# Strassen sums of a second weight matrix made earlier and kept in DRAM, left sums moved to another engine, and another order of seven products

## The chip, the cores and the metric

The kernel runs on one core of one Trainium2 chip. The metric is the device time of one execution in microseconds (us). Engines are named as the profile names them: PE is TensorE (PEld its weight loads), DVE is VectorE, ACT is ScalarE, POOL is GpSimd, SP is SyncE, which here issues nearly all DMAs.

## What is computed

```python
def rmsnorm(x, g):                                  # over the last axis
    return x / np.sqrt(np.mean(x * x, -1, keepdims=True) + 1e-06) * g
q_n, k_n = rmsnorm(q, g_q), rmsnorm(k, g_k)         # q, k, v: (8, 12, 448, 64) float32
attn = softmax(q_n @ k_n.transpose(0, 1, 3, 2) / 8)
x = (attn @ v).transpose(0, 2, 1, 3).reshape(3584, 768)
h = np.maximum(x @ moe_w_in, 0.0)                   # moe_w_in: (768, 2048)
out = (h * h) @ moe_w_out                           # moe_w_out: (2048, 768)
```

Everything is float32. The change concerns the last line, the product with `moe_w_out`, called the out product below, and in it the sums of its right operand (the out weights) and of its left operand (`h * h`).

## The kernel before

**Units.** The eight batches are handled in four units of two. The program runs attention for one unit while it runs the feed-forward of the unit before it, and the last unit's feed-forward runs alone at the end. Unit 0 also brings the weights in and makes their sums. Units 1 and 2 are the middle units (`KEPT`); unit 3 is the last.

**Out product by seven products.** The out product is computed by the Strassen-Winograd scheme: a product of two 2x2 block matrices takes seven block products P1 to P7 instead of eight, at the price of sums of blocks. Left operands are the blocks 11, 12, 21, 22 and the sums S1 to S4, right operands the blocks 11, 12, 21, 22 and T1 = 12 - 11, T2 = 22 - T1, T3 = 22 - 12, T4 = T2 - 21. `PRODUCTS` (line 946) says which left meets which right, and into which PSUM role it goes. The eight right forms of every pair of weight tiles are made once, during unit 0, and kept in DRAM as `out_forms[t]` (one for each of eight tiles), in rows of 384 columns.

**Middle units.** In units 1 and 2 the out product is done once for each of four blocks of the hidden dimension, with one level of the scheme, in `second_products` (line 1230). Its inner loop (line 1315) runs over `SPLIT_ORDER`, 21 products of two matmuls of 128x384. The weights lie in two `out_sb` tiles, loaded by `load_out` (line 924) a few at a time after the block before. Between the products the program goes back to `run` (line 1859), which at each step issues a few of the attention tasks: `tasks` for several engines, `pool_tasks` for POOL (sums of softmax weights, scaling of q, forms of the next unit), DMAs in `transfers`, and in `follow_loads` (line 1805) those DMAs whose count of steps has run out (`later`, `forms_to_load`). Each engine executes its own instructions strictly in the order in which the program issued them, SP its DMAs too. Six accumulators `accs` are allocated for a middle unit, of the seven buffers that the pool has.

**The last unit.** `last_unit` (line 1353) uses the scheme twice, one level inside the other. The outer level is `ROUNDS` (line 1340): seven rounds, one for each outer product, each with one right form (in the order 11, 21, T1, T2, 22, T3, T4), and the plain product with 12 at the end. A round has two half-rounds (`pair` 0 and 1, for two sets of token rows). Each half-round is again seven products, in the order of `ROUND_ORDER` (line 1344), each of four matmuls of 128x192 (line 1578) that go over the four blocks. So each round needs

- the right form, loaded by `load_right` (line 1382) from `out_forms` into `rights[n % 2]` in eight DMAs, issued when the round two before has ended;
- its inner sums, made by `sum_right` (line 1391): T1, T2 and T4 in `more_rights[n % 2]` and T3 in place of the block 12, four subtractions of 768 elements per partition on POOL. The first three are issued at the beginning of the second half of the round before, the fourth at the beginning of the round;
- its outer left sum, if its left operand is one, made a round ahead by `sum_left` (line 1435; which sum in which round says `MADE_IN`): two operations of 1024 elements on VectorE for half 0, two on POOL for half 1, all issued during half 0;
- four inner left sums for every half-round, made by `sum_second` (line 1463) on VectorE, 512 elements each, during the half-round before, one behind each product from the second on.

Each half-round uses three PSUM banks `a, b, c` of one of two sets. P1, P6 and P7 accumulate into a quarter `u_ps` in bank a, P2 goes to the first half of bank b, P5 and P3 to the second half `v_ps` of the same bank, and P4 to bank c. `put` (line 1468) adds a result to an accumulator in SBUF: after P1, P5, P6 and P4 a quarter (192 columns), after P3 the whole of bank b (384), after P7 two quarters at once. The rests, those rows that belong to no half, are done by `multiply_rest` (line 1477) as plain products of 16 records each at the beginning of rounds 0, 1, 4 and at the end. `finish_round` (line 1516) adds two accumulators on POOL after rounds 4 and 5 and stores finished columns; these stores stand in SP's queue with the loads of the right forms.

Of the kernel before, what the change touches and what calls it, by code (L numbers as in the profile page):

```python
# [14 lines left out]
F32 = mybir.dt.float32  # L15
# [8 lines left out]
P = 128  # L24
# [201 lines left out]
def program(ctx, tc, rows, v, g, wide, ones, moe_w_in, moe_w_out, out, shift):  # L226

    nc = tc.nc
# [5 lines left out]
    NF = DFF // P  # L234
    NK = NC // 2
    HALF = DM // 2
# [729 lines left out]
    assert len(KEPT) == 2  # L966
    kept = {u: dram.tile([NBLK, P, 2, 2, P], F32, name=f"rests{u}") for u in KEPT}
# [262 lines left out]
    def second_products(u, blk, hid, sums_, accs):  # L1230

        split = u in KEPT
        if blk == 0:
            accs.extend(new_acc() for _ in range(2 * NT if split else 2 * NT + 1))
# [109 lines left out]
    ROUND_ORDER = ["P1", "P5", "P2", "P6", "P4", "P3", "P7"]  # L1344
# [8 lines left out]
    def last_unit():  # L1353
# [28 lines left out]
        def load_right(n):  # L1382
            if n < len(ROUNDS):
                k = OUT.index(ROUNDS[n][1])
                for t in range(NF // 2):
                    nc.sync.dma_start(rights[n % 2][:, t], out_forms[t][:, k])
# [48 lines left out]
        def sum_left(name, pair, part):  # L1435

            one, other, op = LEFT_SUMS[name]
            engine = nc.gpsimd if pair else nc.vector
            if pair:
                dst, le, ri = [left_of(x, pair, part) for x in (name, one, other)]  # L1440
            else:
                dst, le, ri = [
                    (tokens(x, pair, slice(0, 2 * P)) if x in RAW else summed(x, pair))[:, :, part]
                    for x in (name, one, other)
                ]
            engine.tensor_tensor(out=dst, in0=le, in1=ri, op=op)  # L1446
# [86 lines left out]
        for n, (name, right) in enumerate(ROUNDS):  # L1533
# [9 lines left out]
            sum_right(n, 3)  # L1543
            yield COST_OUT
            for pair in range(2):
# [16 lines left out]
                if pair == 0 and n in MADE_IN:  # L1562
                    extra = deque(partial(sum_left, MADE_IN[n], 0, t) for t in range(2))
                    for t in range(2):
                        sum_left(MADE_IN[n], 1, t)
                else:
# [617 lines left out]
```

## Time and profile before

| what | value |
|---|---|
| median of 3 runs | 1381.4 us (1379.86 to 1383.52) |
| the profiled execution's own time | 1385.1 us |
| its span, first to last instruction | 1383.2 us |
| PE busy | 1344.0 us (97%), 6656 matmul records |
| DVE / ACT / POOL busy | 863.2 / 611.8 / 831.9 us |
| mean granted TensorE clock | 0.995 |
| DMA traffic | 229.88 MB, mean 166 GB/s |
| units 1 and 2, second products and attention among them | 489 to 1090 us |
| rounds of the last unit | 1212.8 to 1371.7 us |

How to read it: one execution on the chip was recorded by the hardware profiler. In the timeline a row has the start, the length, the engine, the line of the kernel, the operation, output and inputs by the program's names, the shapes and how many instructions were merged; in square brackets the idle time of that engine before it and who ended it. A float32 matmul of this kernel shows as two records, so a product of four matmuls is eight records. In a table of stretches each row has the length, the busy time of PE, PEld, DVE, ACT and POOL with their numbers of instructions, the granted clock, the DMA share and GB/s. In the list of waits a row says who waited for whom, for how long in total, how often, and the longest.

### The profile page before, as it was taken

What the parts mean: (1) busy time and instruction counts of PE and PEld (TensorE: products, weight loads), DVE (VectorE), ACT (ScalarE), POOL (GpSimd) and SP (SyncE); (2) the same over time, 40 slices, a digit from 0 to 9 for tenths busy, and PEclk for the clock granted to TensorE, in tenths of its full rate; (3) what the DMA queues carried; (4) which work ended last, traced back from release to release, by engine and by line L of the source; (5) the groups of instructions that cost most, each with busy time, mean ns of one, the idle gap of its engine ahead of it and who ended that gap; (6) DMA issues with size and microseconds to landing.
All of it is one profiled execution on the core that took longest, in us unless ns stands there. A gap on an engine that the chain in (4) does not pass through costs nothing.

```text
span 1383.2 us, 20325 instructions
## 1 busy us (share of the span) xinstructions
PE 1344.0 (97%) x6656; PEld 891.3 (64%) x6656; DVE 863.2 (62%) x1657; ACT 611.8 (44%) x1134; POOL 831.9 (60%) x784
## 2 busy tenths in 40 slices
PE   7999999999999999999999999999999999999897
PEld 3333444444444476776767585766767799978797
DVE  4897555877767765455557665555546645448674
ACT  6985477757756244442534244434424044410000
POOL 5668664746656888566767876665837413146451
PEclk9999999999999999999999999999999999999999
DMA  5665846968769866575649575656535464342222
GB/s 136 165 188 150 204 117 161 260 184 216 239 148 279 244 172 202 153 201 127 206 100 264 148 220 136 181 168 153 166 99 199 137 213 153 96 132 69 91 81 89
DMA packets 399928, 229.88 MB, mean 166 GB/s; under 512 B 272324, under 2 KB 366660, under 8 KB 398788
## 3 DMA queue, kind: packets, MB, share of 16 engines
q1 hardware_dynamic: 399520, 228.41, 58.9%
q8 instruction: 55, 0.90, 0.3%
q14 instruction: 61, 0.50, 0.1%
q10 hardware_dynamic: 292, 0.07, 0.0%
HBM read 171.05 MB, written 57.34 MB: 165 GB/s over the span
## 4 chain that ended last, share of the span: by engine, by line
PE 83%; DVE 6%; issue 3%; POOL 3%; ACT 2%; DMA 2%; SPq 1%; POOLq 0%; ACTq 0%; DVEq 0%
PE bank L1075 25%; PE bank L1272 20%; PE bank L1014 8%; PE bank L1578 8%; PE bank L567 4%; PE bank L449 4%; PE bank L460 4%; PE bank L552 3%; PE bank L1481 1%; PE bank L588 1%; DMA in_sb<-in_deep 1%; PE bank L1214 1%; PE bank L631 1%; DVE left_sums L1446 1%; PE bank L604 1%
## 5 line engine op out<-in xcount | busy, mean ns | idle before, releaser
L1075 PE MATMUL bank<-xT,in_sb 128*128 128x224 f32 x1344 | 287.0, 353 | 0.0
L1075 PEld LDWEIGHTS bank<-xT,in_sb 128*128 128x128 f32 x1344 | 253.1, 190 | 9.4 <-ACT wT L468 5.6
L468 ACT ACTIVATE wT<-bank,rr 128x448 f32<-128x448 f32 x288 | 163.8, 631 | 159.2 <-PE bank L449 98.4
L1272 PE MATMUL bank<-out_sb,hid 128*128 128x384 f32 x576 | 205.6, 489 | 2.1 <-POOL out_sb L1784 1.4
L204 POOL TENSOR_TENSOR rr<-ms,minus_half 128x8 f32<-128x8 f32 (+1 forms) x96 | 145.2, 1512 | 71.5 <-DVE ms L197 61.0
L1615 DVE TENSOR_TENSOR acc<-acc,bank 128x384 f32<-128x384 f32 x231 | 122.5, 546 | 97.8 <-PE bank L1272 77.6
L1272 PEld LDWEIGHTS bank<-out_sb,hid 128*128 128x128 f32 x576 | 108.1, 190 | 80.5 <-issue 7.0
L1272 PE MATMUL bank<-out_sb,sums 128*128 128x384 f32 x432 | 156.0, 491 | 1.4 <-DVE acc L1615 1.0
L1014 PE MATMUL bank<-xT,in_sb 128*128 128x448 f32 x336 | 131.8, 546 | 0.0
L1272 PEld LDWEIGHTS bank<-out_sb,sums 128*128 128x128 f32 x432 | 80.3, 190 | 67.1 <-issue 4.1
L487 POOL TENSOR_TENSOR sum<-sum,wT 128x448 f32<-128x448 f32 (+1 forms) x96 | 112.3, 1191 | 7.5 <-ACT wT L468 6.0
L1014 PEld LDWEIGHTS bank<-xT,in_sb 128*128 128x128 f32 x336 | 62.1, 190 | 68.8 <-issue 61.7
L460 PE MATMUL bank<-qT,kT 64*128 64x448 f32 (+1 forms) x492 | 102.6, 573 | 3.6 <-ACT qT L382 2.5
L1058 DVE TENSOR_TENSOR hid<-hid,bank 128x224 f32<-128x224 f32 x208 | 73.4, 382 | 43.9 <-PE bank L1075 40.5
L487 POOL TENSOR_TENSOR sum<-wT 128x448 f32<-128x448 f32 x48 | 55.9, 1184 | 69.1 <-ACT wT L468 69.1
L460 PEld LDWEIGHTS bank<-qT,kT 64*128 64x128 f32 (+1 forms) x492 | 35.4, 167 | 63.8 <-issue 35.1
L1075 PE MATMUL bank<-more,in_sb 128*128 128x224 f32 x288 | 74.4, 354 | 0.8 <-DVE whole_hid L1058 0.8
L449 PE MATMUL bank<-qT,kT 64*64 64x448 f32 x552 | 75.1, 540 | 0.0
L567 PE MATMUL bank<-wT,vt 64*64 64x448 f32 x576 | 73.3, 545 | 0.0
L382 ACT ACTIVATE qT<-qT,g 128x448 f32<-128x448 f32 x34 | 22.7, 666 | 110.1 <-DVE qT L372 110.1
L1678 ACT ACTIVATE words<-words 128x384 f16<-128x384 f32 x64 | 68.5, 1070 | 2.0
L1058 DVE TENSOR_TENSOR whole_hid<-whole_hid,bank 128x224 f32<-128x224 f32 x104 | 37.9, 386 | 37.1 <-PE bank L1075 35.1
(201 smaller groups left out, 2421.6 us busy)
## 6 DMA issues: line engine op xcount, KB each, us to landing
in_sb<-in_deep SPq DMA_DIRECT2D x64, 384.0 KB, 3.6
in_sb<-in_deep SPq DMA_DIRECT2D x80, 256.0 KB, 3.9
out_sb<-out_forms SPq DMA_DIRECT2D x48, 384.0 KB, 5.2
words<-in_moe_w_in_dram SPq DMA_DIRECT2D x32, 384.0 KB, 3.8
words<-in_moe_w_out_dram SPq DMA_DIRECT2D x32, 384.0 KB, 3.5
out_forms<-out_sb SPq DMA_DIRECT2D x8, 1536.0 KB, 6.6
right<-out_forms SPq DMA_DIRECT2D x64, 192.0 KB, 4.1
qk<-in_q_dram SPq DMA_DIRECT2D x96, 96.0 KB, 2.5
```

The source lines that it names most:

```text
L204: self.nc.gpsimd.tensor_tensor(out=self.rr[i][:, x, 0 : self.count(i)], in0=ms, in1=self.minus_half.to_broadcast(list(ms.shape)), op=ALU.pow,)
L449: nc.tensor.matmul(sc[ds(half * D, D)], lhsT=turned[i, 1][ds(e * D, D), ds(m * P + half * D, D)], rhs=turned[i, 0][ds(e * D, D), :], start ...
L460: nc.tensor.matmul(sc[some], lhsT=turned[p, 1][r, keys], rhs=turned[p, 0][r, :], start=True, stop=True,)
L468: nc.scalar.activation(new_weights((i, m), e), sc, AF.Exp, scale=rows.rr[i][:, 1, 2 * m + e : 2 * m + e + 1],)
L487: nc.gpsimd.tensor_tensor(out=sums[i, e][some], in0=left[some], in1=weights[key_of(i, m), e][some], op=ALU.add)
L567: nc.tensor.matmul(bank[ds(e * D, D), :], lhsT=values[i][keys, n, e, :], rhs=weights[(i, n), e][keys], start=n == 0, stop=n == NJ - 1 and ...
L1014: nc.tensor.matmul(ps, lhsT=w_sb[:, IN.index(left), c, :], rhs=forms[u, c][right], start=first and c == 0, stop=c == NK - 1, skip_group_ch ...
L1058: nc.vector.tensor_tensor(out=quarter(blk, name, n), in0=quarter(blk, base, n), in1=ps, op=ALU.add)
L1075: nc.tensor.matmul(ps, lhsT=left, rhs=right, start=start, stop=stop, skip_group_check=True)
L1272: nc.tensor.matmul(ps, lhsT=lefts[left][:, t, ts(tt, P)], rhs=w_sb[t][:, OUT.index(right), :], start=first and t == 0, stop=t == 1, skip_g ...
L1578: nc.tensor.matmul(ps, lhsT=left[l][:, blk], rhs=rest_of[r][:, blk], start=blk == 0 and product in ("P1", "P5", "P4"), stop=blk == NBLK - ...
L1615: nc.vector.tensor_tensor(out=acc, in0=acc, in1=ps, op=ALU.add)
```

## The change

In the middle units POOL now makes inner sums of the right forms, between the products of a block, and SP stores them in a new DRAM tile `second_forms`: unit 1 does T1 to T4 (four sums for four forms at a time), unit 2 does 21 and 22 (the first three sums for two forms). Each is a subtraction from the `out_sb` tiles into a seventh accumulator buffer, `made`, issued ahead of products 6, 10, 14 and 18 of the order, and its store is issued three steps later. `made` is one buffer, used by all of them in turn.

In the last unit `load_right` loads these sums instead of their being made: three DMAs into `more_rights`, and for T1 to T4 a fourth into the place of the block 12, whose own loads become half as long. POOL's `sum_right` stays for the form 11 (three sums, during the products before the rounds), and the fourth sum of 11, 21 and 22 is made on VectorE. `sum_left` is done on VectorE for both halves, in four pieces of 512 elements per half-round, in the same list of jobs as `sum_second`; two jobs are issued behind a product where the list is too long for one. And `ROUND_ORDER` has P4 and P2 exchanged.

```diff
+    second_forms = dram.tile([P, 8, 4, NBLK, HALF // 2], F32, name="second_forms")
...
-            accs.extend(new_acc() for _ in range(2 * NT if split else 2 * NT + 1))
+            accs.extend(new_acc() for _ in range(2 * NT + 1))
...
+        def sum_second_forms(n):
+
+            q = HALF // 2
+            some = (ds(4, 4), ds(2, 2))[KEPT.index(u)]
+            size = (4, 2)[KEPT.index(u)]
+            made = accs[-1][:, 0 : size * q].rearrange("p (k c) -> p k c", k=size)
+            b11, b12, b21, b22 = [w[:, some, ts(h, q)] for w in w_sb for h in range(2)]
+            left, right = ((b12, b11), (b22, made), (made, b21), (b22, b12))[n]
+            less(nc.gpsimd, made, left, right)()
+            later.append([3, partial(nc.sync.dma_start, second_forms[:, some, n, blk], made)])
...
-            for name, tt, n in SPLIT_ORDER:
+            for at, (name, tt, n) in enumerate(SPLIT_ORDER):
+                if at in (6, 10, 14, 18)[: 4 if u == KEPT[0] else 3]:
+                    sum_second_forms((at - 6) // 4)
...
-    ROUND_ORDER = ["P1", "P5", "P2", "P6", "P4", "P3", "P7"]
+    ROUND_ORDER = ["P1", "P5", "P4", "P6", "P2", "P3", "P7"]
...
         def load_right(n):
-            if n < len(ROUNDS):
-                k = OUT.index(ROUNDS[n][1])
-                for t in range(NF // 2):
-                    nc.sync.dma_start(rights[n % 2][:, t], out_forms[t][:, k])
+            if n >= len(ROUNDS):
+                return
+            name = ROUNDS[n][1]
+            k, to = OUT.index(name), rights[n % 2]
+            for t in range(NF // 2):
+                some = slice(0, HALF if t % 2 or name in RAW else Q)
+                nc.sync.dma_start(to[:, t, some], out_forms[t][:, k, some])
+            if name in ("11", "12"):
+                return
+            for m in range(3):
+                nc.sync.dma_start(more_rights[n % 2][:, m], second_forms[:, k, m])
+            if name not in RAW:
+                nc.sync.dma_start(right_of(n, 0, 1), second_forms[:, k, 3])
...
-            less(nc.gpsimd, dst, left, right)()
+            less(nc.vector if m == 3 else nc.gpsimd, dst, left, right)()
...
-        def sum_left(name, pair, part):
-
+        def sum_left(name, pair, i, t):
             one, other, op = LEFT_SUMS[name]
...
+            dst, le, ri = [left_of(x, pair, i)[:, :, t] for x in (name, one, other)]
+            nc.vector.tensor_tensor(out=dst, in0=le, in1=ri, op=op)
...
-            sum_right(n, 3)
+            if right in RAW:
+                sum_right(n, 3)
...
-                if pair == 0 and n in MADE_IN:
-                    extra = deque(partial(sum_left, MADE_IN[n], 0, t) for t in range(2))
-                    for t in range(2):
-                        sum_left(MADE_IN[n], 1, t)
-                else:
-                    extra = deque()
-                if pair and n + 2 < len(ROUNDS):
-                    for m in range(3):
-                        sum_right(n + 1, m)
-                for product in ROUND_ORDER:
+                if n in MADE_IN:
+                    jobs.extend(
+                        partial(sum_left, MADE_IN[n], pair, i, t) for i in range(2) for t in range(2)
+                    )
+                for slot, product in enumerate(ROUND_ORDER):
...
-                    if extra:
-                        extra.popleft()()
-                    elif jobs and product != "P1":
-                        jobs.popleft()()
+                    for _ in range(2 if len(jobs) > 6 - slot + 1 else 1):
+                        if jobs:
+                            jobs.popleft()()
```

More of the change, by code (lines that the diff above doesn't have):

```diff
@@ L1433, in left_of @@
             return tokens(name, pair, some)
-        def sum_left(name, pair, part):
+        def sum_left(name, pair, i, t):
             one, other, op = LEFT_SUMS[name]
-            engine = nc.gpsimd if pair else nc.vector
-            if pair:
-                dst, le, ri = [left_of(x, pair, part) for x in (name, one, other)]
-            else:
[L1442 to L1446, printed above, removed]
+            dst, le, ri = [left_of(x, pair, i)[:, :, t] for x in (name, one, other)]
+            nc.vector.tensor_tensor(out=dst, in0=le, in1=ri, op=op)
         rounds = [(n, pair) for n in range(len(ROUNDS) - 1) for pair in range(2)]
@@ L1561, in last_unit @@
                     jobs.extend(partial(sum_second, at + 1, x) for x in LEFT_SUMS)
-                if pair == 0 and n in MADE_IN:
-                    extra = deque(partial(sum_left, MADE_IN[n], 0, t) for t in range(2))
-                    for t in range(2):
-                        sum_left(MADE_IN[n], 1, t)
-                else:
-                    extra = deque()
-                if pair and n + 2 < len(ROUNDS):
-                    for m in range(3):
-                        sum_right(n + 1, m)
-                for product in ROUND_ORDER:
+                if n in MADE_IN:
[3 more added lines that the diff above has]
+                for slot, product in enumerate(ROUND_ORDER):
                     role, first, l, r = PRODUCTS[product]
```

## The prediction

> **What bounds the kernel now.** I read the page first, then the stretches and TensorE's waits of the two middle units, then the last unit in order of time.
>
> ```profile
> PE 1344.0 (97%) x6656; PEld 891.3 (64%) x6656; DVE 863.2 (62%) x1657; ACT 611.8 (44%) x1134; POOL 831.9 (60%) x784
> ```
>
> TensorE is busy in 1344.0 of 1383.2 us. An edit pays only where TensorE is idle or slow, and costs only where it makes TensorE wait. The middle units (489 to 1090 us) first: the stretches (length, then busy time of each engine; the sum is over 16 of them) and everything TensorE waited for there.
>
> ```profile
> 753.00:789.50 36.50, 35.73 (x157) 19.33 (x159) 27.52 (x49) 11.10 (x21) 31.75 (x38) 1.00 0.64 181
> ...
> sum 593.60, PE 591.15 PEld 418.63 DVE 338.92 ACT 232.50 POOL 406.14; mean PE 36.95 PEld 26.16 DVE 21.18 ACT 14.53 POOL 25.38
> ```
>
> ```profile
> PE bank L1075 <- DVE hid L1058: 1.2, 3, 0.6
> PE bank L1272 <- DVE acc L1615: 0.6, 1, 0.6
> PE bank L1272 <- ACT acc L1611: 0.4, 2, 0.2
> ```
>
> TensorE is idle for 593.60 - 591.15 = 2.45 us there, and never because of POOL. Nothing can be won in the middle units; something can be lost.
>
> Now the last unit's seven rounds: 14 half-rounds of seven products, each product four matmuls, which the trace shows as eight records. This sum row covers the three stretches in which only they run (the whole-row products of L1481 cut out):
>
> ```profile
> sum 148.59, PE 135.96 PEld 131.82 DVE 106.09 ACT 5.62 POOL 79.49; mean PE 45.32 PEld 43.94 DVE 35.36 ACT 1.87 POOL 26.50
> ```
>
> A slow half-round and an ordinary one, TensorE in order of time (start, length, what ended an idle time before it):
>
> ```profile
> 1237.53 1.46 PE L1578 MATMUL bank<-right,whole_hid 128*128 128x192 f32 x8
> 1238.83 1.46 PE L1578 MATMUL bank<-more_right,qk 128*128 128x192 f32 x8
> 1242.63 2.93 PE L1578 MATMUL bank<-right,whole_hid 128*128 128x192 f32 x8 [2.34 <-DVE acc L1475]
> 1245.35 1.78 PE L1578 MATMUL bank<-more_right,qk 128*128 128x192 f32 x8
> ...
> 1342.29 1.46 PE L1578 MATMUL bank<-right,left_sums 128*128 128x192 f32 x8
> 1343.59 1.46 PE L1578 MATMUL bank<-more_right,second_sums 128*128 128x192 f32 x8
> 1345.50 1.57 PE L1578 MATMUL bank<-right,left_sums 128*128 128x192 f32 x8 [0.45 <-DVE acc L1475]
> 1346.90 1.46 PE L1578 MATMUL bank<-more_right,second_sums 128*128 128x192 f32 x8
> ...
> 1352.10 1.46 PE L1578 MATMUL bank<-right,whole_hid 128*128 128x192 f32 x8
> ```
>
> One product takes 1343.59 - 1342.29 = 1.30 us, so seven take 9.12 (7 x 1.302). The ordinary half-round takes 1352.10 - 1342.29 = 9.81. The missing 0.69 lies at the third product, P2, which starts 1345.50 - 1343.59 = 1.91 after P5 instead of 1.30, and is itself 0.1 slow. P2 writes the first half of the bank whose second half P5 has just filled, and starts only when VectorE has emptied that half. In the slow half-round the same P2 starts 3.80 us after P5, for the reason that VectorE's rows show:
>
> ```profile
> 1239.30 3.02 DVE L1446 TENSOR_TENSOR left_sums<-whole_hid,whole_hid 128x1024 f32<-128x1024 f32 x1
> 1242.24 0.34 DVE L1475 TENSOR_TENSOR acc<-acc,bank 128x192 f32<-128x192 f32 x1
> ...
> 1286.33 1.21 DVE L1446 TENSOR_TENSOR left_sums<-whole_hid,left_sums 128x1024 f32<-128x1024 f32 x1
> 1287.47 0.34 DVE L1475 TENSOR_TENSOR acc<-acc,bank 128x192 f32<-128x192 f32 x1
> ...
> 1340.16 0.68 DVE L1466 TENSOR_TENSOR second_sums<-left_sums 128x512 f32<-128x512 f32 x1
> 1341.19 0.55 DVE L1475 TENSOR_TENSOR acc<-acc,bank 128x384 f32<-128x384 f32 x1 [0.34 <-PE bank L1578]
> ```
>
> ```profile
> 1237.13 1.80 POOL L744 TENSOR_TENSOR right<-right 128x768 f32<-128x768 f32 x1 [15.57 <-PE bank L1481]
> 1238.89 2.34 POOL L1446 TENSOR_TENSOR left_sums<-whole_hid,whole_hid 128x1024 f32<-128x1024 f32 x1
> 1241.20 3.32 POOL L1446 TENSOR_TENSOR left_sums<-rest_left,rest_left 128x1024 f32<-128x1024 f32 x1
> ```
>
> The eviction that P2 needs (1242.24) stands behind a left sum of 1024 elements, and that sum takes 3.02 us while POOL works on its own left sums, against 1.21 (1286.33) while POOL rests. The evictions themselves, with one input from PSUM, take 0.34 both times. And a long gap costs twice:
>
> ```profile
> 1242.60:1246.90 4.30, 4.27 (x16) 4.27 (x17) 4.30 (x2) 0.00 (x0) 4.30 (x2) 0.61 0.02 4
> ```
>
> After the gap of 2.34 us the granted clock is 0.61 for 4.3 us: P2 takes 1245.35 - 1242.63 = 2.72 instead of 1.30, and the next product is 1.78 long instead of 1.46, together about 1.7 us lost behind the gap.
>
> **Part by part.** *The order (P1, P5, P4, P6, P2, P3, P7).* P4 has a bank of its own, so the third product waits for nothing. P6 adds to P1's bank, P2 to P5's; each now has two products (2.60 us) between it and the fill of its bank, where P2 had none. P7 keeps two behind P6. If VectorE empties P1's and P5's quarters within 2.60 us of their end, all seven products run without a gap: 14 x 9.12 = 127.7 us in place of 148.59, which is 20.9 us less. Of this, 14 x 0.69 = 9.7 is the order alone, and 11.2 are the slow half-rounds.
>
> *VectorE's new load.* In the eight half-rounds of rounds 1 to 4 it gets four left sums of 512 elements beside its four second-level sums of 512 (0.68 each, row 1340.16). With four small evictions at 0.34 and two of 0.55 that is 8 x 0.68 + 1.36 + 1.10 = 7.9 us of 9.12; in the other six 5.2. In order, counted from the start of P1: the last eviction and job of the half-round before end at 1.4, P1's eviction at 1.9 (needed at 3.9), two sums by 3.2, P5's at 3.6 (needed at 5.2), a sum by 4.2, P4's by 4.6, a sum by 5.2, P6's at 5.8 (needed at 7.8). Every one is early by 1.6 us or more. The one subtraction on the right operand that stays (rounds 0, 1, 4) goes from POOL to VectorE: 768 elements, by the 512 row about 1.0 us. It waits for L1481 to have read that operand; behind it on VectorE are only evictions of products that start after L1481. It costs nothing; its result is due at P7, 7.8 us later.
>
> *POOL in the last unit* loses its left sums and all but the first three right sums, so the 3.02 us of row 1239.30 should fall to the undisturbed price. Four additions of accumulators stay, and each may hold one VectorE sum for some 1.8 us (row 1237.13 has the same size); the 1.6 us margin above nearly takes that. I set it at nothing.
>
> *Loads of the right operand.* Per round before:
>
> ```profile
> 1231.63 3.65 SPq L1386 DMA_DIRECT2D right<-out_forms  x8
> ```
>
> ```profile
> right<-out_forms SPq DMA_DIRECT2D x8, 192.0 KB, 3.8
> ```
>
> Eight issues in 3.65 us, the last landing 3.8 later: 1.57 MB in 7.5 us. After, a round of T1 to T4 brings 4 x 192 + 4 x 96 + 4 x 384 KB = 2.75 MB in 12 issues, one of 21 or 22 brings 2.75 MB in 11. At the same rate that is 13.1 us. They start when the round two before ends and are due one whole round, 18.2 us, later. 5 us to spare: no cost.
>
> *The middle units.* POOL gets 4 x 4 subtractions of 768 elements (1.80, row 1237.13) and 4 x 3 of 384 (half of that): 28.8 + 10.8 = 39.6 us. Each result is stored by SP, and each next one waits for that store, since all use one buffer. Behind a waiting subtraction on POOL stand the scaling of keys, the sums of the softmax weights and the forms for the next unit; behind a store that waits for POOL on SP stand loads of q, k, v, in_sb and out_sb. Who waits for those at last is TensorE. Over the 16 stretches POOL is idle for 593.60 - 406.14 = 187 us, so most of it fits. The tightest place is the end of unit 1:
>
> ```profile
> 774.19 0.93 POOL L643 COPY few<-few 32x14 f32<-32x14 f32 x4 [3.22 <-DVE few L641]
> ...
> 792.35 2.84 POOL L744 TENSOR_TENSOR xT<-xT 128x224 f32<-128x224 f32 x3
> ```
>
> ```profile
> 800.61 0.54 PE L1075 MATMUL bank<-more,in_sb 128*128 128x224 f32 x2
> ```
>
> ```profile
> out_sb<-out_forms SPq DMA_DIRECT2D x48, 384.0 KB, 5.2
> ```
>
> POOL has 36.50 - 31.75 = 4.75 us idle in that block; four subtractions are 7.2, so its forms come at least 2.5 us later. They are done at 795.2 at the latest and read at 800.61: 5.4 us of slack. No wait there is the low end. If the three waits for stores (5.2 us as a block of 384 KB, 0.4 to issue) were all uncovered, the lag would be 2.5 + 16.8 = 19.3 and TensorE would stand 13.9 us: the high end. A gain is excluded, as TensorE never waits for POOL there. Other POOL work lies between the subtractions and covers most of each store, so I stay by the first row: 1.5 us in all for the eight blocks.
>
> Sum: -20.9 + 1.5 = -19.4 us. The profiled execution took 1385.1 (span 1383.2); it would take 1365.7. It lies 3.7 above the median, so against the median of 1381.4: 1362.0.
>
> **The rivals.** *A stall between the units:* POOL's lag passes the slack by 5 us at one place. Priced by the row of the clock, such a gap adds 1.7 us behind it: 6.7 more than the sum without middle costs, 1360.5 + 6.7 = 1367.2, and twice that is 1373.9. For it: POOL's 31.75 of 36.50. Against: slack 5.4. The Trainium skill ("TensorE: Matmul & The Clock Gate", What's actually happening) has the clock fall only after an idle window of about 3.4 us; the row shows it at 0.61 after 2.34, so the measurement decides. By that rule a stall under 3.4 us would cost its own length alone.
>
> *VectorE becomes the bound:* if the eight fuller half-rounds take 10.5 instead of 9.12 (sums at 1.0 instead of 0.68), 8 x 1.4 = 11.2 of the gain is gone: 1373.2. Against it stands the undisturbed 0.68.
>
> *The order does not do it:* the wait moves from P2 to P6 or P2 at its new place, 14 x 0.69 = 9.7 lost: 1371.7. Against it: two products of cover against an eviction that is done 0.6 us after its product.
>
> *Slower:* the whole added POOL time in the middle units reaches TensorE, block by block: 1362.0 - 1.5 + 39.6 = 1400. It decides from 20.9 / 8 = 2.6 us of stall per block. For it: one buffer and an SP queue in strict order. Against: 187 us of idle POOL.
>
> **How the numbers follow.** Forecast 0.70, stall 0.13, VectorE 0.05, order 0.04, slower 0.05, and 0.03 for a mix of these that ends near the time before. A measurement of this kernel can tell 0.3%, 4.1 us, from no change. Faster by more: 0.92 (the first four); within: 0.03; slower: 0.05. The range: 1358.5 is the full 20.9 with no cost, less 2 us for the spread of the three runs (1379.86 to 1383.52); 1371.0 is 9 us above the forecast, which takes in one stall, some two thirds of the 13.9 us bound, and leaves out VectorE, order, slower and mix, 0.17 in all.
>
> **What would show it.** Right: no idle time before the fifth or third product of a half-round, half-rounds of 9.12 us, granted clock 1.00 through the rounds, left sums near 0.68, POOL almost empty after 1210 us, and TensorE's waits in the middle units near 2.45 us. Wrong: waits of L1075 or L631 for POOL near 795, waits of L1578 for right or more_right, or for VectorE at P6 and P2.

## The result, and the profile after

The changed kernel takes 1368.0 us (median of 4 runs, 1367.6 to 1368.8) against 1381.9 before (median of 4, 1379.9 to 1383.5): a ratio of 0.990, interval 0.988 to 0.992. That is faster by 13.9 us, where 19.4 had been forecast.

From the page of the changed kernel, the busy times and, from the costliest groups, VectorE's evictions in the middle units (busy time and mean ns behind the first bar, idle time before them behind the second). The line numbers have moved: L1578 is now L1589, L1481 is L1496, L1475 is L1490, L1272 is L1273, L1615 is L1625, and the inner left sums of L1466 are at L1481.

```profile
PE 1336.1 (98%) x6656; PEld 887.1 (65%) x6656; DVE 850.8 (62%) x1684; ACT 612.4 (45%) x1134; POOL 798.9 (58%) x779
...
L1625 DVE TENSOR_TENSOR acc<-acc,bank 128x384 f32<-128x384 f32 x231 | 122.7, 547 | 99.5 <-PE bank L1273 79.9
```

The profiled execution took 1368.14 us with a span of 1366.3, which is 16.9 us less span than before. TensorE is busy for 7.9 us less, and VectorE's evictions still take 547 ns on average.

**The last unit.** The stretch from the whole-row product ahead of the first half-round to the end of the last half-round, with three whole-row products (3 x 5.16 us) in it; the columns are length, busy time of PE, PEld, DVE, ACT and POOL, granted clock, DMA share, GB/s:

```profile
1212.40:1355.10 142.70, 142.70 (x833) 136.34 (x832) 90.72 (x161) 8.50 (x23) 7.88 (x4) 1.00 0.50 160
```

TensorE is busy for all of the 142.70 us at a clock of 1.00. The trace has fourteen half-rounds of 9.10 us each, 127.4 us in all where before had 148.59: 21.2 less. POOL does four additions there and nothing else. A half-round and the beginning of the next, at the place where the prediction showed a slow one:

```profile
1240.78 1.46 PE L1589 MATMUL bank<-right,whole_hid 128*128 128x192 f32 x8
1242.08 1.46 PE L1589 MATMUL bank<-more_right,qk 128*128 128x192 f32 x8
1243.38 1.46 PE L1589 MATMUL bank<-more_right,whole_hid 128*128 128x192 f32 x8
...
1247.28 2.76 PE L1589 MATMUL bank<-right,qk 128*128 128x192 f32 x16
1249.88 1.46 PE L1589 MATMUL bank<-right,whole_hid 128*128 128x192 f32 x8
```

```profile
1240.33 0.96 DVE L744 TENSOR_TENSOR right<-right 128x768 f32<-128x768 f32 x1 [3.96 <-DMA more_right<-second_forms]
1242.28 0.35 DVE L1490 TENSOR_TENSOR acc<-acc,bank 128x192 f32<-128x192 f32 x1 [0.98 <-PE bank L1589]
...
1245.15 0.69 DVE L1481 TENSOR_TENSOR second_sums<-whole_hid,rest_left 128x512 f32<-128x512 f32 x1
1246.45 1.28 DVE L1461 TENSOR_TENSOR left_sums<-whole_hid,whole_hid 128x512 f32<-128x512 f32 x2
```

The seven products follow each other every 1.30 us (two are merged at 1247.28), from 1240.78 to 1249.88, and no row carries a bracket. VectorE is ahead of TensorE (its eviction waits 0.98 us for TensorE), its sums take 0.69 and, two merged, 1.28. Its own wait of 3.96 us for the load of the inner sums is harmless here: the fourth sum behind it is due at P7, and no product waits.

**The middle units.** There the time came back. TensorE's waits from 680 to 800 us (in total, times, longest):

```profile
PE bank L1273 <- DVE acc L1625: 3.7, 1, 3.7
PE bank L1273 <- DMA out_sb<-out_forms: 1.1, 1, 1.1
PE bank L1076 <- DVE hid L1059: 0.7, 1, 0.7
```

The last block of products of unit 1, which lasted from 755.0 to 789.5 us before, lasts from 753.9 to 794.0:

```profile
753.90:794.00 40.10, 35.21 (x149) 18.71 (x148) 29.54 (x46) 9.59 (x18) 36.66 (x39) 0.96 0.59 174
```

That is 40.1 us where 34.5 had been enough, 5.6 us more. Set beside the trace of before, matmul by matmul, no other block of the middle units is longer: TensorE is 1.1 us ahead of before when this block begins, 4.6 us behind when it ends, and still 4.6 behind at the rounds. What happened at 784 us is told by three engines:

```profile
784.29 1.45 PE L1273 MATMUL bank<-out_sb,hid 128*128 128x384 f32 x4
789.49 2.91 PE L1273 MATMUL bank<-out_sb,sums 128*128 128x384 f32 x4 [3.74 <-DVE acc L1625]
```

```profile
783.64 0.54 DVE L1625 TENSOR_TENSOR acc<-acc,bank 128x384 f32<-128x384 f32 x1
784.11 4.86 DVE L744 TENSOR_TENSOR more<-xT 128x224 f32<-128x224 f32 x1
788.90 0.54 DVE L1625 TENSOR_TENSOR acc<-acc,bank 128x384 f32<-128x384 f32 x1
```

```profile
783.66 1.13 POOL L710 TENSOR_TENSOR xT<-xT,inverse 128x448 f32<-128x448 f32 x1
784.75 1.80 POOL L744 TENSOR_TENSOR acc<-acc,out_sb 128x768 f32<-128x768 f32 x1
786.51 2.21 POOL L744 TENSOR_TENSOR xT<-xT 128x448 f32<-128x448 f32 x2
788.68 1.47 POOL L204 TENSOR_TENSOR rr<-ms,minus_half 128x6 f32<-128x6 f32 x1
```

Read them from the bottom. POOL multiplies attention's output by the inverse of the softmax sums (L710), then makes the third of the new sums (`acc<-acc,out_sb`, 1.80 us), then two more subtractions, with no gap between. VectorE starts a small subtraction of 224 elements at 784.11, while L710 runs. In the trace of before the same one takes 0.38 us:

```profile
785.73 0.38 DVE L744 TENSOR_TENSOR more<-xT 128x224 f32<-128x224 f32 x1
```

Here it takes 4.86 and ends at 788.97, 0.25 us after POOL's last subtraction. Behind it on VectorE stands the eviction that frees TensorE's next bank, and TensorE is idle for 3.74 us. The gap is followed by a slow clock (columns as above):

```profile
790.00:795.00 5.00, 5.00 (x20) 2.29 (x22) 3.40 (x8) 0.67 (x1) 4.92 (x6) 0.70 0.08 13
```

At 0.70 the product behind the gap takes 2.7 us instead of 1.3, and the next one 0.4 more than usual: 1.8 us. With the 1.1 us for a load of the out weights, the block should be longer by 3.7 + 1.1 + 1.8 = 6.6, less the 0.77 us (36.50 - 35.73) that TensorE was idle around it before: 5.8, where 5.6 are measured.

### The profile page after: what moved, and what is told of

It reads as the page before. It is cut to its first block, busy times and chain, and to the rows that moved or that the text cites. A ratio compares the mean times of both kernels' runs of the same rounds, so it can differ in the third digit from the quotient of the medians.

```text
span 1366.3 us, 20405 instructions
## 1 busy us (share of the span) xinstructions
PE 1336.1 (98%) x6656; PEld 887.1 (65%) x6656; DVE 850.8 (62%) x1684; ACT 612.4 (45%) x1134; POOL 798.9 (58%) x779
## 4 chain that ended last, share of the span: by engine, by line
PE 87%; DVE 3%; POOL 3%; ACT 2%; issue 2%; DMA 1%; SPq 1%; POOLq 0%; DVEq 0%; ACTq 0%
PE bank L1076 25%; PE bank L1273 21%; PE bank L1589 9%; PE bank L1015 8%; PE bank L460 4%; PE bank L567 4%; PE bank L449 4%; PE bank L552 3%; PE bank L1496 2%; PE bank L588 1%; PE bank L604 1%; PE bank L1215 1%; PE bank L631 1%; PE bank L622 1%; POOL sum L487 1%
## 5 line engine op out<-in xcount | busy, mean ns | idle before, releaser
L1273 PE MATMUL bank<-out_sb,hid 128*128 128x384 f32 x576 | 206.0, 490 | 3.1 <-POOL out_sb L1794 1.4
L1625 DVE TENSOR_TENSOR acc<-acc,bank 128x384 f32<-128x384 f32 x231 | 122.7, 547 | 99.5 <-PE bank L1273 79.9
L1273 PEld LDWEIGHTS bank<-out_sb,hid 128*128 128x128 f32 x576 | 108.3, 190 | 82.1 <-issue 9.0
L1273 PE MATMUL bank<-out_sb,sums 128*128 128x384 f32 x432 | 157.0, 494 | 4.2 <-DVE acc L1625 3.7
L1273 PEld LDWEIGHTS bank<-out_sb,sums 128*128 128x128 f32 x432 | 81.0, 191 | 69.6 <-issue 6.0
L1536 POOL TENSOR_TENSOR acc<-acc 128x768 f32<-128x768 f32 x2 | 4.3, 2134 | 106.3 <-DVE acc L1490 106.3
```

The costliest lines, as they stand in the source:

```text
L1273: nc.tensor.matmul(ps, lhsT=lefts[left][:, t, ts(tt, P)], rhs=w_sb[t][:, OUT.index(right), :], start=first and t == 0, stop=t == 1, skip_g ...
L1625: nc.vector.tensor_tensor(out=acc, in0=acc, in1=ps, op=ALU.add)
```

## The experiments

Ratios and gains are each against runs of the kernel before on the same chip.

### The rounds: which part of the change does it

**order_only** is the kernel before with the new order alone.

```diff
-    ROUND_ORDER = ["P1", "P5", "P2", "P6", "P4", "P3", "P7"]
+    ROUND_ORDER = ["P1", "P5", "P4", "P6", "P2", "P3", "P7"]
```

> The kernel before with the new order of products and nothing else. Theory (the order frees the third product of its wait, the slow half-rounds come from VectorE and POOL working at once): the nine ordinary half-rounds lose their 0.69 us, 6.2 us; the five slow ones stay bound by VectorE, where some 0 to 4 us more may go because evictions have two products of cover. About 1373 to 1376. Rival (all waits of the rounds are the one wait at the third product, so the order alone brings everything): about 1361. Second rival (the wait only moves): 1382.

Measured: 1370.7 us, ratio 0.9915 (0.9898 to 0.9931), 11.6 us faster. The rounds take 136.0 us, 12.6 less than before, and ten of the fourteen half-rounds are at 9.1 us already. (The expectation counted nine ordinary half-rounds and five slow ones in the trace of before; there are ten and four.) From one of the other four, the fifth, the sixth and the seventh product (P2, P3, P7) on TensorE, and VectorE's rows around them:

```profile
1239.68 1.48 PE L1578 MATMUL bank<-right,whole_hid 128*128 128x192 f32 x8
1241.00 1.46 PE L1578 MATMUL bank<-right,qk 128*128 128x192 f32 x8
1245.19 2.90 PE L1578 MATMUL bank<-right,qk 128*128 128x192 f32 x8 [2.73 <-DVE acc L1475]
```

```profile
1236.25 3.02 DVE L1446 TENSOR_TENSOR left_sums<-whole_hid,whole_hid 128x1024 f32<-128x1024 f32 x1
...
1242.76 2.02 DVE L1466 TENSOR_TENSOR second_sums<-rest_left 128x512 f32<-128x512 f32 x1
1244.70 0.34 DVE L1475 TENSOR_TENSOR acc<-acc,bank 128x192 f32<-128x192 f32 x1
```

VectorE is as slow here as before. But P2 no longer waits; only at the end of the half-round is VectorE so late that P7 stands 2.73 us for P6's eviction. The order hides not only its own 0.69 us but also part of VectorE's lateness, which is why it gave more than expected: not in this half-round (13.40 us, 13.34 before), but in the other three that were slow before, which take 2.1, 2.0 and 2.5 us less.

**undo_order** is the changed kernel with the old order.

```diff
-    ROUND_ORDER = ["P1", "P5", "P4", "P6", "P2", "P3", "P7"]
+    ROUND_ORDER = ["P1", "P5", "P2", "P6", "P4", "P3", "P7"]
```

> The changed kernel with the old order of products. Theory: the third product waits again for the eviction of the second in all 14 half-rounds, 14 x 0.69 = 9.7 us, and in the eight half-rounds with two sums behind the first product that eviction stands 0.4 us later: 1368.0 + 9.7 + 3.2 = 1381 at most, 1377.7 at least. Rival (the gain is POOL's absence alone): 1368.

Measured: 1384.8 us, ratio 1.0011 (1.0000 to 1.0022), more than was expected. Two products at the old place:

```profile
1293.47 1.46 PE L1589 MATMUL bank<-more_right,second_sums 128*128 128x192 f32 x8
1295.68 1.57 PE L1589 MATMUL bank<-right,left_sums 128*128 128x192 f32 x8 [0.74 <-DVE acc L1490]
```

P2 starts 2.21 us after P5 (before: 1.91), because VectorE now makes two sums behind P1, ahead of P5's eviction. In the profiled execution the rounds take 143.2 us, 5.4 less than before, but they start 4.8 later, and next to nothing is left. Without the order the rest of the change is worth nothing.

**order_left** is order_only with the left sums on VectorE as in the change, while POOL still makes the right sums.

```diff
-            engine = nc.gpsimd if pair else nc.vector
...
-            engine.tensor_tensor(out=dst, in0=le, in1=ri, op=op)
+            dst, le, ri = [left_of(x, pair, i)[:, :, t] for x in (name, one, other)]
+            nc.vector.tensor_tensor(out=dst, in0=le, in1=ri, op=op)
...
+                if n in MADE_IN:
+                    jobs.extend(
+                        partial(sum_left, MADE_IN[n], pair, i, t) for i in range(2) for t in range(2)
+                    )
```

> The kernel before with the new order and the left sums of both halves on VectorE in pieces of 512; the right sums stay on POOL and nothing is done in the middle units. Theory (any POOL work with SBUF inputs slows VectorE's sums): 28 right sums of about 2 us on POOL stretch VectorE's sums, in rounds 1 to 4 by up to 8 us per round where 2.4 us are free, so a part of the 11.2 us of the slow half-rounds stays, some 3 to 8 us, but the stall of 5.7 us in unit 1 is not there: 1364 to 1369, near the changed kernel. Rival (only the left sums matter, the margin of two products hides the rest): 1361 to 1362, faster than the changed kernel.

Measured: 1369.9 us, ratio 0.9906 (0.9889 to 0.9922), just above the range expected. The rounds take 134.5 us, 1.4 less than with the order alone, and the half-round that was slow in order_only still takes 12.15. POOL's left sums are gone and VectorE is as slow as ever:

```profile
1237.43 1.95 DVE L1458 TENSOR_TENSOR second_sums<-rest_left 128x512 f32<-128x512 f32 x1
1239.42 2.18 DVE L1458 TENSOR_TENSOR second_sums<-second_sums,whole_hid 128x512 f32<-128x512 f32 x1
1241.52 0.34 DVE L1467 TENSOR_TENSOR acc<-acc,bank 128x192 f32<-128x192 f32 x1
```

```profile
1237.02 1.81 POOL L744 TENSOR_TENSOR more_right<-right 128x768 f32<-128x768 f32 x1
1238.91 2.14 POOL L744 TENSOR_TENSOR more_right<-right,more_right 128x768 f32<-128x768 f32 x1
```

A sum of 512 elements takes 2 us instead of 0.69, each about as long as the right sum that POOL makes beside it. It is not the length of VectorE's list: the changed kernel has the same left sums on VectorE and a right sum more, and its half-rounds take 9.1.

**order_right** is the other half: the changed kernel (right sums from DRAM, new order) with the left sums as they were, two large ones on VectorE and two on POOL.

```diff
-                if n in MADE_IN:
-                    jobs.extend(
-                        partial(sum_left, MADE_IN[n], pair, i, t) for i in range(2) for t in range(2)
-                    )
+                if pair == 0 and n in MADE_IN:
+                    extra = deque(partial(sum_left, MADE_IN[n], 0, t) for t in range(2))
+                    for t in range(2):
+                        sum_left(MADE_IN[n], 1, t)
```

> The changed kernel with the left sums as before: half 0 on VectorE in pieces of 1024, half 1 on POOL at the same time. Theory: in the first half-rounds of rounds 1 to 4 two left sums of 3.05 us instead of 1.21 and POOL beside the second sums give VectorE 11 us of work for 9.12, about 2 us lost in each, some of it hidden by the two products of cover: 1371 to 1377. Rival (the right sums were the whole trouble): 1368.

Measured: 1370.0 us, ratio 0.9903 (0.9880 to 0.9926). All fourteen half-rounds take 9.1 us, 127.4 in all, as in the changed kernel; the 2 us per half-round that my theory expected did not show. VectorE's left sums now have their undisturbed price:

```profile
1245.99 1.22 DVE L1469 TENSOR_TENSOR left_sums<-whole_hid,whole_hid 128x1024 f32<-128x1024 f32 x1
```

So it was the right sums on POOL that made VectorE slow, by themselves (order_left) and by holding POOL's left sums back until VectorE made its own. Freed from standing behind them, POOL's left sums run in this trace at other times than VectorE's, but for one (1.77 us instead of 1.22, at 1282.39), and TensorE waits for none. The move of the left sums gives nothing measurable once the right sums are gone.

**order_again** repeats order_only on another chip, beside the changed kernel.

> The order of products alone, once more beside the changed kernel on one chip, to tell what the rest of the change brings. By the traces the rest wins 136.0 - 127.4 = 8.6 us in the rounds and loses 6.3 before them, 2.3 us in all: 1370.5. If the rest brings nothing: equal to the changed kernel.

Measured: 1372.1 us, ratio 0.9926 (0.9912 to 0.9939), rounds 135.9. The changed kernel on the same chip (after_again, below) took 1368.3. So what the change has beside the order is worth 3.8 us net: 8.5 won in the rounds and nearly 6 lost in one block of unit 1 by the traces; the remaining 1 us lies within the spread of executions.

### The block of unit 1: what costs the time there

**skip_four** leaves POOL's four subtractions out in this one block.

```diff
-            less(nc.gpsimd, made, left, right)()
+            if not (u == KEPT[0] and blk == NBLK - 1):
+                less(nc.gpsimd, made, left, right)()
```

> The changed kernel without the four subtractions of the last block of unit 1; their stores stay and store what the buffer held, so the sums of that block are not computed. Theory (the stall of TensorE at 785 to 792 us is VectorE held by an unbroken run of POOL instructions in which a subtraction lies): it goes, about 5 to 5.7 us, 1362.5. Rival (the stores and the SP queue behind them cost the time): 1368, unchanged.

Measured: 1364.2 us, 1.7 above the expected, ratio 0.9857 (0.9837 to 0.9876). The wait for VectorE is down to the 0.6 us of before. The profiled execution was the slowest of the four (1366.2): in it the wait for the load of the out weights was 2.0 us with a slow clock behind, and the block was still 3.5 us longer than before. So this load is late without POOL's sums, too.

**skip_third** leaves out only the third of the four, the one that stands between L710 and the two subtractions.

```diff
-            less(nc.gpsimd, made, left, right)()
+            if not (u == KEPT[0] and blk == NBLK - 1 and n == 2):
+                less(nc.gpsimd, made, left, right)()
```

> The changed kernel without the third of these four subtractions only, the one that lies in POOL's run between 783.7 and 788.7 us; its store stays, and the sum is not computed. Theory of the run: VectorE's subtraction is held until the end of a run that is 1.8 us shorter, so TensorE stands 1.9 instead of 3.7 us, and perhaps without the fall of the clock: 1365 to 1366.5. Rival (POOL is late by all four subtractions): a quarter of the loss, 1366.7 at best, with the same gap at the same place.

Measured: 1363.4 us, ratio 0.9850 (0.9830 to 0.9870). TensorE's wait for VectorE is gone whole, more than expected, and the block is 0.6 us longer than before. (The profiled execution was again the slowest, 1366.8: it lost 1.9 us to a late load of `in_sb` at 829 us, and more to the slow clock behind it.) VectorE's row and POOL's there:

```profile
784.70 0.93 DVE L744 TENSOR_TENSOR more<-xT 128x224 f32<-128x224 f32 x1
```

```profile
784.26 1.12 POOL L710 TENSOR_TENSOR xT<-xT,inverse 128x448 f32<-128x448 f32 x1
785.35 2.51 POOL L744 TENSOR_TENSOR xT<-xT 128x448 f32<-128x448 f32 x2
```

The subtraction starts while L710 runs, as in the changed kernel, and ends at 785.63, 0.25 us after L710, although POOL goes on without a gap. One POOL instruction of 1.8 us decides whether VectorE's takes 0.93 or 4.86.

**units_swapped** lets unit 1 make the smaller sums (21 and 22) and unit 2 those of T1 to T4.

```diff
-            some = (ds(4, 4), ds(2, 2))[KEPT.index(u)]
-            size = (4, 2)[KEPT.index(u)]
+            some = (ds(2, 2), ds(4, 4))[KEPT.index(u)]
+            size = (2, 4)[KEPT.index(u)]
...
-                if at in (6, 10, 14, 18)[: 4 if u == KEPT[0] else 3]:
+                if at in (6, 10, 14, 18)[: 3 if u == KEPT[0] else 4]:
```

> The changed kernel with the units exchanged: unit 1 makes the three sums of 21 and 22 (384 elements), unit 2 the four of T1 to T4 (768), which has more idle POOL time in its last block. Theory of the run: the subtraction in the run before the unit's end is half as long, the stall about 0.9 us shorter, and unit 2 may get one of its own: 1365 to 1368. Rival (POOL's lateness at the end of unit 1): the stall goes, 1362.

Measured: 1366.5 us, ratio 0.9875 (0.9856 to 0.9895). The same place has a smaller gap:

```profile
786.86 1.56 PE L1273 MATMUL bank<-out_sb,sums 128*128 128x384 f32 x4 [2.13 <-DVE acc L1625]
```

```profile
781.95 3.09 DVE L197 TENSOR_SCALAR ms<-ms 128x6 f32<-128x6 f32 x1
```

With the third sum half as long (1.00 us), the instruction that happens to be caught is an operation on 6 elements with one input, and it takes 3.09 us: from L710 over the third sum to the end of the first of the two subtractions.

**swapped_right** is units_swapped with the left sums as before (the edit of order_right on top).

```diff
-            some = (ds(4, 4), ds(2, 2))[KEPT.index(u)]
+            some = (ds(2, 2), ds(4, 4))[KEPT.index(u)]
...
+                if pair == 0 and n in MADE_IN:
+                    extra = deque(partial(sum_left, MADE_IN[n], 0, t) for t in range(2))
```

> Units exchanged, and the left sums of the last unit as before the change (half 1 on POOL, pieces of 1024). The rounds took 127.4 us without any gap with the left sums in either place, so this should equal units_swapped within 1.5 us. Rival (left sums on POOL matter): 3 us or more above it.

Measured: 1365.7 us, ratio 0.9870 (0.9850 to 0.9890), rounds 127.4. That is 0.7 us from units_swapped, which confirms order_right: the place of the left sums makes no difference that can be measured here.

**later_spots** is the changed kernel with the third and fourth sum of this block two products later, behind the two subtractions.

```diff
-                if at in (6, 10, 14, 18)[: 4 if u == KEPT[0] else 3]:
-                    sum_second_forms((at - 6) // 4)
+                spots = (6, 10, 16, 20) if u == KEPT[0] and blk == NBLK - 1 else (6, 10, 14, 18)
+                if at in spots[: 4 if u == KEPT[0] else 3]:
+                    sum_second_forms(spots.index(at))
```

> The changed kernel, but in the last block of unit 1 the third and fourth subtractions are issued ahead of products 16 and 20 instead of 14 and 18, so that POOL's two subtractions for the next unit come between. The work is the same. Theory of the run: VectorE is no longer held across the third subtraction, the gap of 3.7 us and the slow clock behind it go: 1362.5 to 1364.5, like the kernel that leaves the third out. Rival (the work itself, or its stores, costs the time wherever it stands): 1368.

Measured: 1366.3 us, ratio 0.9890 (0.9874 to 0.9907). In the trace of the block it does what was expected: VectorE's subtraction is short again, and TensorE waits for neither VectorE's evictions nor the load. The row:

```profile
784.62 0.93 DVE L744 TENSOR_TENSOR more<-xT 128x224 f32<-128x224 f32 x1
```

The block is 1.0 us shorter than before, but 1.0 is lost again right behind it (from 788.85 to 795.54 us, 6.7 us for work that took 5.7 before), and 0.9 more by 830. The profiled execution took 1365.0; two of the other three took 1367.4 and 1367.7, and no trace of these was kept. By its median the edit is 2 us worse than expected, and its interval overlaps that of the changed kernel on this chip (0.9888 to 0.9920): the trace shows that the wait goes, the times do not show the gain.

**swapped_later** puts the third sum of unit 1's last block later in units_swapped as well.

```diff
-                if at in (6, 10, 14, 18)[: 3 if u == KEPT[0] else 4]:
-                    sum_second_forms((at - 6) // 4)
+                spots = (6, 10, 16, 20) if u == KEPT[0] and blk == NBLK - 1 else (6, 10, 14, 18)
+                if at in spots[: 3 if u == KEPT[0] else 4]:
+                    sum_second_forms(spots.index(at))
```

> Units exchanged, and in the last block of unit 1 the third subtraction ahead of product 16. Theory: the remaining gap of 2.1 us there goes as well: 1362 to 1364. Rival: as with the units exchanged alone, 1365.5 to 1366.5.

Measured: 1364.9 us, ratio 0.9883 (0.9866 to 0.9900): 17.0 us faster than the kernel before, 0.9 above the expected range, and by its median 3.4 faster than the changed kernel on the same chip, though its slowest execution (1367.4) comes near that one's fastest (1368.0). TensorE's only wait of 680 to 800 us in its profiled execution, and the block:

```profile
PE bank L1076 <- DVE hid L1059: 0.6, 1, 0.6
```

```profile
753.10:788.00 34.90, 34.80 (x155) 19.00 (x153) 26.26 (x47) 10.26 (x19) 31.56 (x37) 1.00 0.61 177
```

The stretch holds the block, which is down from 40.1 us to 33.5 (754.5 to 788.0 in the trace), with its three sums of 384 elements in it, at a clock of 1.00.

**after_again** is the changed kernel once more, on the chip of the last four.

> The changed kernel once more, beside the order alone: 1368.0; the difference to it 2.3 us by the traces, 0 if the rest of the change brings nothing.

Measured: 1368.3 us, ratio 0.9904 (0.9888 to 0.9920). The same 3.7 us wait for VectorE at the same place, and 1.3 for the load. The gap belongs to the program, not to one execution: undo_order and order_right, which make the same sums, have it as well, 3.7 us each.

## Why the prediction was right, and where it was off

Faster was right, and 1368.0 lies in the range; the forecast of 1362.0 was 6.0 too low. Two terms account for that, the middle units and the step from one execution to the median. By the prediction's own steps.

**Order and slow half-rounds.** The sum of -20.9 us came out at -21.2. Its split did not: 9.7 for the order and 11.2 for the slow half-rounds were predicted, order_only shows 12.6 and leaves 8.6. And the slow half-rounds were put down to POOL's left sums; order_left and order_right show that POOL's right sums are at the bottom of it. The change takes both away, so the sum held in spite of the wrong reason; that is luck.

**VectorE's new load, the right operand's loads, POOL's four additions.** Each was set at nothing, and each cost nothing: no wait of TensorE in the rounds, sums at 0.69 (0.68 predicted), the fourth sum at 0.96 (1.0 predicted).

**The middle units.** This is the mis-sized term: 1.5 us predicted, 5.6 in a single block measured. It lay within the bounds of 0 to 13.9, but the mechanism was another one. I had reckoned with late forms of POOL, with its waits on the one buffer `made` and with SP's waits on POOL's sums. Those waits exist (SP's are 46.2 us over 15 stores), but in the middle units no wait of TensorE is put down to POOL:

```profile
POOL acc L744 <- DMA second_forms<-acc: 12.1, 7, 3.3
```

What did reach TensorE was VectorE, held up by POOL. The prediction had the row for this (3.02 us instead of 1.21 beside POOL) and used it in the last unit alone. Moving POOL's sums out of the last unit moved that contention into the middle units, and there I priced it at nothing. The list of waits of before even had a trace of it: TensorE's 0.6 us for VectorE at this place stands behind an operation on 6 elements (L197, at 784.04 us) that took 1.31 us beside POOL, against 0.17 undisturbed. Skip_third removes the wait by removing one sum, later_spots and swapped_later by moving it; that makes this cause shown for the wait and the slow clock behind it. The 1.1 us for the load of the out weights is another matter. It is seen in the changed kernel both times (1.1, 1.3), in undo_order and order_right (1.2, 1.5), and in skip_four and skip_third (2.0, 1.7), not in units_swapped or later_spots; order_again, which makes no sums there, has 0.5 of it. In the changed kernel SP issues no store of the new sums between 735 and 769 us, so the load, issued at 757.6, does not stand behind one. Why it is late stays open.

**The rival of a stall between the units** had one place, a gap of 5 us with 1.7 for the clock, 6.7 in all. The place was the same block or the border behind it, the gap 3.7 with 1.8 for the clock, so its size was nearly right; POOL's lag, its reason, was wrong.

**From one execution to the median.** The profiled execution was to take 1365.7 and took 1368.1. The terms: -0.3 in the rounds, +4.1 in the middle units, -1.1 in unit 0, which the change does not touch, and -0.3 in the tail behind the rounds make +2.4. The other 3.6 us come from the base: the profiled execution of before lay 3.7 above its median, that of after 0.1 above. I had assumed that the distance would stay. The record says where most of it comes from. Of the 30 executions of the kernel before with a clock on record, the nine with a mean granted clock of 0.995 took 1384.9 to 1385.9 us, the one with 0.996 took 1384.0, and the twenty with 0.997 or 0.998 took 1379.7 to 1383.4. The profiled one has 0.995, and its trace shows three falls of the clock in the rounds, behind three of the slow half-rounds' gaps; the products behind them lost some 5 us (1.7 + 1.8 + 1.6). Those 5 us are within the 11.2 of the slow half-rounds, which the change takes away. Taking the 3.7 off as well counted most of them twice. That the other executions had fewer falls at the same gaps is inferred from their mean clock; they have no trace.

**The clock.** The prediction priced a gap by the row with 0.61 after 2.34 us. The length of the gap alone does not decide: behind 2.13 us (units_swapped) a product took the usual time, behind a shorter gap in the trace of before it was slow:

```profile
1255.52 2.29 PE L1578 MATMUL bank<-right,whole_hid 128*128 128x192 f32 x8 [1.89 <-DVE acc L1475]
1257.60 2.46 PE L1578 MATMUL bank<-more_right,second_sums 128*128 128x192 f32 x8
```

The granted clock itself shows a pattern. In the trace of before it falls at 1242.56, 1256.22 and 1314.24 us, 4 and 17 times 3.413 us apart, and stays at 0.50 for 3.41 us each time. Here are the 3.41 us ahead of the second fall and those behind it, then the stretch of units_swapped that holds most of the gap of 2.13 us (columns as above):

```profile
1252.80:1256.21 3.41, 1.52 (x10) 1.22 (x9) 3.41 (x5) 0.00 (x0) 3.41 (x2) 1.00 0.10 36
1256.22:1259.63 3.41, 3.41 (x13) 3.41 (x12) 3.38 (x2) 0.00 (x0) 3.22 (x2) 0.50 0.22 78
```

```profile
785.25:788.66 3.41, 1.80 (x6) 1.14 (x7) 3.38 (x8) 0.00 (x0) 3.33 (x4) 1.00 0.71 141
```

TensorE is idle for 3.41 - 1.52 = 1.89 us in the first and for 3.41 - 1.80 = 1.61 in the last, because that gap lies across the border at 785.25. Divide every one of the fourteen traces into such windows of 3.413 us, from the clock's first rise (17.2 us in before) to the window before the one in which the last matmul ends: from the full clock it falls behind each window with 1.86 us of idle time or more, and behind none with 1.75 or less. (Ends of matmuls are modelled, so this border is known to a tenth or two; in the last window 1.97 once passed without a fall.) A gap of 3.74 us has 1.87 in one window wherever it lies, and all four kernels that have it show the fall; a gap of 2 us is slow or not by where it lies. The Trainium skill ("TensorE: Matmul & The Clock Gate", What's actually happening) has such a window of about 3.4 us, running freely, and would have the clock fall after an idle one. The traces agree on the window; that it must be idle throughout, 1.86 (undo_order), 1.89 (before) and 1.94 us (skip_third) decide against here.

**Open.** The traces don't say what sets how long POOL holds VectorE: it was one POOL instruction in skip_third and later_spots, three in units_swapped and four in the changed kernel, and POOL's rows show no gap in any of them. Also open in part are the 2 to 4 us by which executions of swapped_later and later_spots differ. In swapped_later the mean clock goes with it: 1.000 in the two faster ones (1362.8 and 1364.4), 0.998 in the two slower (1365.4 and 1367.4); 0.002 of 1365 us is about 2.7.

## What to carry to other kernels

When work on POOL is moved to another stage, look there for VectorE's instructions that read SBUF alone and for the evictions queued behind them; free time on POOL says nothing about what its instructions do to VectorE. Before buying back a slow helper with memory and transfers, try the order of the consumers: one line here, which puts two products between a bank's fill and its next use, gave 11.6 us on one chip and 9.8 on another, of the 13.5 to 13.9 of the whole. And when the profiled execution lies off the median by as much as the terms at stake, look first at what makes it so (here its mean granted clock): if the change removes that, the distance goes with it and must not be taken off a second time.

## What the runs showed of the hardware

- VectorE's instruction on 224 elements went from 0.38 to 4.86 us beside four POOL instructions in a row, and one on 6 elements with a single input took 3.09 us. The evictions, which read PSUM and SBUF, stayed at 0.54. The Trainium skill ("SBUF — State Buffer", Who interferes with whom) has VectorE and GpSimd share a port pair, which whoever comes first keeps for the whole instruction. The traces agree in that VectorE's instruction ended 0.25 us after the end of one of POOL's, in the changed kernel and in skip_third; but 4.86 us span more than the one instruction of 1.13 us that POOL had begun.
- Two accumulation targets in the two halves of one bank cost this program 0.69 us per half-round when the second product follows the first directly, since it waits for VectorE's eviction of the other half; with two products (2.6 us) between they cost nothing.
- The granted clock fell to 0.50 for 3.41 us (twice that in order_only and order_right) behind fixed windows of 3.41 us in which TensorE was idle for 1.86 us or more, and cost about 1.7 us each time in the rounds of before.
- 15.7 MB more of DMA traffic (229.9 to 245.6 MB), loads of the rounds among it, made no wait of TensorE in the rounds.
